# Batch 2's queries and keys turned by transposing DMAs instead of TensorE, with a new order of all engines

## The chip, the cores and the metric

The kernel runs on one core of one Trainium2 chip. The metric is the device time in microseconds (us) of one execution. Engines are named as the profile names them: PE is TensorE's matmul stream and PEld its weight loads, DVE is VectorE, ACT is ScalarE, POOL is GpSimd (which here only issues loads from HBM), SP is SyncE (which issues the other DMAs).

## What is computed

An attention with a local window and a few global keys, and behind it a gated long convolution that takes its result as input. There are B = 4 batches, 8 heads, S = 768 positions and D = 64 values per head; the first 8 keys are seen by every query, and beside them each query sees itself and the 95 keys before it. The masked scores carry a bias that falls with distance, with a slope for each head.

```python
scores = scale * np.matmul(q, k.transpose(0, 1, 3, 2))
...
keep = is_global | is_local
dist = np.where(is_global & ~is_local, float(n_local), np.abs(rel))
scores = np.where(keep, scores - slopes[:, None, None] * dist, -1e9)
a = np.exp(scores - max); a = a / sum(a)
x = (a @ v), heads joined to 512 columns
...
proj = x @ w_proj                       # 512 -> 3 * 512
x1, x2, x3 = the three parts of proj
x2_conv = irfft(rfft(x2, axis=1) * rfft(filter_fft, axis=0))
out = (x1 * x2_conv * x3) @ w_out
```

The lines above are shortened; inputs are cast to 16-bit floats on the way in and the output is 32-bit.

## The kernel before, in words

**Attention of one batch.** The scores need queries and keys with the 64 values of a head on the partitions, while they lie in HBM with positions in the rows. They are loaded as rows and then turned. `QT` (line 759 reads it, with `KT`) holds the turned queries, 128 rows for each pair of heads; `KT` holds seven key tiles of 8 global and 120 local keys each. `scores` (L741) makes, for a pair of heads and one of three groups of key tiles, the scores in two PSUM banks; ACT takes their exponential (L774) and DVE multiplies with a mask that holds the bias and the window (L791). `values` (L794) multiplies with the values, which carry a column of ones for the sum; DVE takes the reciprocal, and DVE or ACT scales the result into `xn` (L833 on DVE; L837 on ACT, one small instruction for each tile and head). `transpose_x` (L843) turns it on PE (L854), and DVE or ACT copies it out of PSUM to `xT` (`copy`, L314).

**Gated convolution of one batch.** `gate` (L922) makes two of the projections (L932), `butterfly` (L861) folds `xT`, `conv` (L981) projects (L993) and carries the transform by matmuls with tables (`spectra` L1117, L1124; back at L1023), and the output projection (L1059) goes by ACT to `ot` and from there by SP to HBM (L1070).

**Two ways to turn queries and keys.** Batches 1 and 2 go the first way, batch 3 the second; batch 0 goes a variant of the first.

- On PE: `load_pair` (L358) loads, head by head, 96 KB at a time, so 16 loads for a batch. `turned` (L697) makes six 128x128 transposes of a head pair into one bank (L707), and then a copy by ACT or DVE brings it out: one copy of 128x768 for queries, and three for keys (128x720, 128x120, and 128x56 for the global ones). A batch has four pairs, so eight such steps and 48 transposes.
- By DMA: `load_tiles` (L379) loads rows of all heads, six query tiles of 128 KB and seven key tiles of 120 KB, and two SP copies (kn<-kn) repeat the eight global keys in every tile. `cross` (L396) then issues 13 transposing DMAs on SP (L406), one for a tile, which write `QT` and `KT` directly. The names are TILES and CROSS; both are (3,).

`QT`, `KT` and the row buffers `qn`, `kn` exist once, the value buffer `vn` twice. So rows of batch b + 1 can only be loaded where rows of batch b were turned, and `QT` and `KT` only be written where the scores of the batch before were made. `load_v` (L411) loads the values in seven row tiles; when the first of them is there, `load_global` (L418) copies its eight global rows to the other tiles with two DMAs on SP (vn<-vn), which `values` waits for.

**Order.** Every operation is recorded with its engine or engines, its cost and what it reads and writes. `schedule` (L156) then takes the order from a string written out by hand: each word is the number of an operation, the letter of its engine (P, A, V for DVE, G for POOL, S for SP) and its PSUM banks. `248G` is the load of the first value tile of batch 1, `249S` the copy of its global rows. Where an operation may go to ACT or DVE, the letter decides. Each engine runs its words in that order, and a word that waits holds up the words of its engine behind it. DMAs too are issued in the order of POOL's and of SP's words.

Of the kernel before, what the change touches and what calls it, by code (L numbers as in the profile page):

```python
# [17 lines left out]
P = 128  # L18
# [23 lines left out]
0V 1V 2A 3G 45S 30A 47S 4V 34V 6A 9A 32G 56S 49S 5V i1b5 22P0 55G 23A 54G 7G 24A 10V 17P1 8V 33V 25V 51G 18A  # L42
35G 19A 12P2 13A 46V 52G 37A 48V i2b5 83P0 38A 53G 81P3 72G 20V 26A 61G 63G 21A 14V 44V 50V 15V 39V 201P1 93P2
36V 87P4 84A 202V 57V 60G 43A 82A 207V 95P3 16A 94A 97P67 209V 85P2 65G 64G 29V 11V 62G 88A 41V 91P0 203V 66G
96V 149P45 239G 42A 236G 86V 98A 204A 234G 150A 40V 89P3 121P67 151P45 238G 58V 208V 90V 205V 122A 152A 117P23
92V 99P67 206V 103P45 211V 233G 212V 118A 213V 235G 100A 119P23 101P67 153P01 104A 105P45 120A 102A 154A 27V
214V 115P23 237G 106V 215V 59S 116A 107V 155P67 78A 216V 110P01 111V 128P23 232G 157P45 156A 77A 217V 67G
220P6 112V 162P01 221A 158V 108P6 73A 113P7 129V 130V 123P23 109A 224P6 159V 131P4 114V 79A 222P7 245G 68G
341P5 241G 243G 225A 163V 124V 76A 223A 218P6 31V 240G 164V 125V 337P0 132V 28V 339P1 244G 340V 165P7 126P4
127V 247G 160P2 74A 335P1 338A 137P4 342A 166V 193V 139A 161V 133P7 376P23 219A 242G 336V 246G 354P45 414P01  # L50
377A 138P6 69G 167P2 355A 134P3 415A 183V 135A 184V 351P45 352A 192V 194V 140V 373P01 186V 185V 136V 343P6
374A 459G 169A 248G 195V 172P7 70G 71G 171P4 464G 187V 196V 173A 226P01 347P2 227A 345P3 411P45 251G 344V 252G
353V 349P0 145P6 75A 174V 249S 412A 348V 141P2 346V 254G 357P45 350V 228A 417P01 147A 375V 253G 420P67 188V
168P3 255G 197V 458G 256G 470G 356V 189V 143A 170V 142P2 465G 418A 471G 144V 175P0 358A 146P1 421A 382P67 198V
191V 460G 360P23 177A 413V 199V 148V 80A 190V 383A 379P45 380A 258P0 463G 361A 259A 229P67 416V 200V 378V
271P1 363P45 272A 230A 422V 275P2 461G 364V 273P3 231A 250S 466G 276A 284P6 419V 385P01 362V 274A 384V 286P7
359V 260P2 386V 365V 387V 462G 560P3 287A 479G 478G 285A 469G 261A 368P45 381V 279P0 366P1 472G 561A 473G 369V
468G 277P2 288V 423P67 370V 280A 262P3 289V 264P0 278A 367A 371P1 424V 263A 467G 425V 372A 282V 566P2 428P45
266P1 390P67 257G 265A 706G 567A 562P0 281V 267A 429V 388P3 391V 563A 179P2 430V 564P1 392V 176P4 181A 180P0
565A 389A 269V 576P67 268V 182V 178V 426P1 577A 431P2 393P0 432V 427A 394V 579P45 687G 580A 598P67 639P23 640A  # L60
396P0 698G 572P1 574P4 270V 395P5 298P2 407P3 696G 573A 599A 474G 397A 450V 570P1 568P6 449V 451V 695G 452V
404P5 575A 299A 408P7 694G 409A 403P4 571V 684G 398V 636P23 585P01 453V 410V 690G 569A 283V 454V 405A 600V
637A 582P67 445P4 480G 586A 481G 699S 399P2 447A 406V 433P3 446P4 455V 477G 702G 292P5 583A 435A 401A 456V
457V 645P67 607P01 448V 693G 293A 300P3 638V 646A 290P2 294P5 441P4 295A 304P6 442P5 581V 476S 608A 482G 584V
443A 400P7 475S 578V 302P4 697G 296P0 609V 688G 301A 291A 647V 303A 444V 689G 402V 485P1 604P45 297A 305A 587V
642P23 486A 307V 306V 605A 601P67 641V 691G 643A 685S 483P0 496P1 593P23 602A 308V 594V 603V 497A 484A 498P4
606V 588P67 487P5 589V 683G 701G 499A 595A 437P4 309V 489P0 590V 490A 488A 704G 310V 615P67 439A 692G 644V
311V 703G 610P23 611V 616V 700S 653P01 491P5 617A 438P4 612V 312V 511P2 440V 654V 686S 434P3 313V 596P4 618P6
512A 597A 492A 619A 500P7 655V 591P2 592A 613P5 314V 493V 501A 502P4 509P6 494V 648P01 504P7 656P2 705G 614A
624P5 510A 787S 649V 505A 513V 657A 632P6 503A 436V 315V 620P7 507V 629P4 621P3 626A 323P5 495V 506V 789S 514V  # L70
625P2 650A 508V 785S 634A 622A 651P0 324A 652A 628P6 784S 515P7 786S 517P5 529P1 518A 623V 527P3 627V 316V
675V 523P0 516A 528A 519P2 630A 670P5 525P3 793S 526A 521P7 633P6 530A 520A 791S 332P3 674V 317P2 524A 635V
333A 631V 672A 662P3 522A 803P45 790S 677V 806P67 800P01 318A 664A 801A 788S 676V 326P2 804A 795S 532V 327A
329P3 320P0 678V 330A 321A 796S 707P2 679V 663P3 807A 797P01 531V 680V 794S 825P67 533V 708A 534V 822P45 798A
682V 826A 720P2 666P0 535V 805V 536V 665V 671P3 823A 537V 681V 828P67 673V 721A 819P45 711P1 658P3 668A 820A
712A 799V 792S 829A 724P2 861P01 827V 870P67 660A 867P45 725A 722P3 540V 538V 802V 319S 334S 871A 733P2 868A
539V 723A 709P6 809P45 726P3 541V 734A 808V 554P7 331S 872V 810V 727A 735P3 542P2 830V 811V 862A 863V 555A
710A 814P01 836P45 864P67 736A 815V 543A 824V 837V 667P3 816V 865A 659P2 869V 838A 866V 715P6 713P7 661V
878P01 325S 669V 714A 548P2 728P7 812P3 879V 716A 821V 880V 737V 817P6 831P45 729A 873P01 839P7 322S 832V 730V
818A 813A 874V 551P3 731V 833A 875V 328S 732V 718V 557P6 881P4 738V 834P5 876P0 545P1 840A 835A 882A 877A  # L80
856P7 556S 717V 841P4 904V 741P0 903V 719V 745P5 546A 749P1 558A 742A 843A 549A 746A 857P6 842P0 906V 905V
907V 908V 851P2 858A 909V 750A 753P7 559S 844A 747P5 754A 739P4 743P1 751P0 883P7 744A 912P1 748A 910V 740A
852P4 752A 756V 859A 755V 913A 924P6 853A 936P2 552A 925A 911V 884P5 757V 854A 938P6 914P3 845V 937A 758V
916P2 939A 915A 860V 928P3 759V 888P6 210A 917A 760V 553S 940V 761V 929A 920P4 550S 918P3 886A 919A 926P2 941V
764V 921A 923V 922V 932P3 889P5 927A 898P4 933A 930P3 544S 894P2 885A 946P7 931A 762V 896A 942P3 935V 957P1
846P2 934V 855V 947A 958A 961P7 943A 944P1 962A 948P3 945A 763V 959P0 949A 963P7 960A 964A 765V 951V 950V
847P1 781P0 547S 891A 965V 966V 952V 967V 769P5 899P7 848A 953V 770A 900A 968V 954V 969V 772P2 955V 970V 956V
766P3 849A 773A 971V 850V 974V 774S 901A 972V 893P2 767A 782A 975V 775P7 973V 890A 892V 778P3 771S 895A 897V
982P2 768S 985V 779A 902V 783S 976P3 887V 776A 979P7 986V 983A 987V 993P2 989P6 988V 780S 994P 1001P0 980V
990P 777S 977A 978S 997P7 998P 995A 984S 991A 999A 1002P 1003V 981S 996S 992S 1000S 1004S  # L90
# [24 lines left out]
class Plan:  # L115
# [7 lines left out]
    def op(self, eng, cost, fn, r=(), w=(), acq=(), use=(), nbytes=0, table=None, name="",  # L123
# [21 lines left out]
        for b in use:  # L145
            b.left += 1
            b.users.append(o)
            p.add(b.owner)
# [50 lines left out]
class Fused:  # L199
# [6 lines left out]
    PAIR_G = ()  # L206
    VD = 96
    FIRST = (("k",0),("q",0),("k",1))
    TILES = (3,)
    CROSS = (3,)  # L210
# [27 lines left out]
    def buffers(self):  # L238
# [35 lines left out]
        self.ab = [t(f"ab{i}", [P, 3, DM]) for i in range(2)]  # L274
        self.X = t("X", [P, 6, DM])
        pp = t("pp", [P, 2, 4, DM])
        self.p1, self.p2 = ([pp[:, x, 2 * i:2 * i + 2] for i in range(2)] for x in range(2))
# [9 lines left out]
        self.ot = [t(f"ot{i}", [P, DM], F32) for i in range(6)]  # L287
# [555 lines left out]
    def transpose_x(self, j, c):  # L843
# [5 lines left out]
        def run(_):  # L849
            tx = b.f16()  # L850
            for i in range(2):
                for n, t in enumerate(ts):
                    o = step * i + KL * n
                    nc.tensor.transpose(tx[:, o:o + P], self.xn[j][:, i, t], self.ident)  # L854
        g.op("P", 0.0558 * 2 * len(ts), run, acq=[b], r=[("xn", j, c), "ident"], name="trx")
        dst = self.xT[:, 2 * j:2 * j + 2, self.Q0[c]:self.Q0[c] + W]
        g.op("AV", {"A": act(2 * W), "V": dve(2 * W, 2, True)}, lambda e: self.copy(
            e, dst, b.f16()[:, 0:2 * step].rearrange("p (i w) -> p i w", i=2)[:, :, 0:W]), use=[b],
            w=[("xT", j, c)], name="xT")
# [89 lines left out]
    def attention(self, b):  # L949
# [5 lines left out]
        for c in range(3):  # L955
# [8 lines left out]
            for j in range(2):  # L964
                self.values(j, c, b % 2)
                self.transpose_x(j, c)
# [14 lines left out]
    def conv(self, b):  # L981
        nc, g, DM, S = self.nc, self.g, self.DM, self.S
        h, last = S // 2, b == self.B - 1
        g.batch = (self.PERIOD * b, self.PERIOD)
        X, y, w = self.X, self.y, self.w
        for i in range(2):
            for t, (src, key) in enumerate((
                    (self.xo[:, i], ("xo",)), (self.xs[:, 3 * i], ("xe", "xd")), (self.xs[:, 2 - i], ("xe", "xd")))):
                bk = g.bank()
# [308 lines left out]
```

## Time and profile before

| | us |
|---|---|
| median of 3 runs | 165.75 |
| lowest, highest | 165.38, 165.85 |
| span of the profiled execution | 163.0 |
| median less that span | 2.75 |
| PE busy | 154.0 |
| DVE busy | 151.6 |
| ACT busy | 150.3 |
| POOL busy | 76.8 |

The profiled execution has no other time of its own than its span. Busy time of PE counts a matmul until its modelled end, so PE at 10 of 10 us needn't be PE at its peak. The page names groups of instructions by source line and by tiles: `KT<-bank` is a copy from a PSUM bank to `KT`. Issues of DMAs on POOL and SP have their own rows; "us to landing" is from the issue to the last byte. Queue q0 carries POOL's DMAs and q1 SP's.

### The profile page before, as it was taken

To read this page: it belongs to the slowest core of one execution; us is meant where nothing else is said; L and a number is where in the kernel's file an instruction comes from. 1 tells how busy PE (TensorE), PEld (TensorE's weight loads), DVE (VectorE), ACT (ScalarE), POOL (GpSimd) and SP (SyncE) were. 2 spreads that over 40 slices of the span, in tenths; PEclk is the share of its full clock that TensorE was granted. 3 is DMA by queue.
4 is the path that set the end of the run, shared out by engine and by line. 5 is a ranking of instruction groups with operands and counts; after the bars stand their busy time and mean duration, and the time that the engine had idled before them with its cause. 6 is when DMAs were issued, how large, how long until landed. Compare 5 with 4: busy or idle time off the path is not lost.

```text
span 163.0 us, 4256 instructions
## 1 busy us (share of the span) xinstructions
PE 154.0 (94%) x1604; PEld 94.7 (58%) x1604; DVE 151.6 (93%) x356; ACT 150.3 (92%) x327; POOL 76.8 (47%) x101
## 2 busy tenths in 40 slices
PE   6599997999999999999999999999999999999980
PEld 2274355866655777666577584445676664584440
DVE  6599699999999999999999999999999999999960
ACT  8999996999999999999999999999998999997850
POOL 7999199999979997999970000000000000000000
PEclk9999999999999999999999999999999999999999
DMA  5999999999999999999999964630100106000684
GB/s 170 200 166 164 165 150 138 147 158 174 190 162 154 139 136 136 149 153 163 161 129 162 134 121 101 236 150 0 64 4 6 66 0 253 5 4 0 264 332 178
DMA packets 84956, 21.95 MB, mean 135 GB/s; under 512 B 75584, under 2 KB 81992, under 8 KB 84936
## 3 DMA queue, kind: packets, MB, share of 16 engines
q0 software_dynamic: 73040, 12.11, 98.4%
q1 hardware_dynamic: 11896, 9.57, 21.4%
q8 instruction: 12, 0.20, 0.5%
q14 instruction: 8, 0.07, 0.1%
HBM read 25.40 MB, written 6.29 MB: 194 GB/s over the span
## 4 chain that ended last, share of the span: by engine, by line
PE 85%; ACT 9%; DVE 3%; issue 1%
PE bank L932 26%; PE bank L993 13%; PE bank L1059 13%; PE bank L759 7%; PE bank L854 4%; PE bank L809 4%; PE bank L707 3%; PE bank L1023 3%; PE bank L1124 3%; PE bank L814 3%; PE bank L753 2%; ACT E L774 2%; ACT KT L314 1%; PE bank L1030 1%; PE bank L690 1%; ACT QT L314 1%
## 5 line engine op out<-in xcount | busy, mean ns | idle before, releaser
L932 PE MATMUL bank<-xT,w 128*128 128x384 f16 x256 | 48.2, 326 | 0.0
L774 ACT ACTIVATE E<-bank 128x864 f16<-128x864 f32 x48 | 41.0, 911 | 0.3 <-PE bank L759 0.2
L932 PEld LDWEIGHTS <-w 128*128 128x128 f16 x256 | 23.9, 98 | 15.8 <-issue 0.3
L339 POOL DMA_DIRECT2D vn<-in_v_dram x28 | 26.3, 979 | 1.1 <-DMA w<-in_moe_w_proj_dram 1.1
L339 POOL DMA_DIRECT2D kn<-in_k_dram x25 | 21.8, 892 | 5.4 <-DMA vn<-in_v_dram 4.0
L1059 PE MATMUL bank<-wo,y 128*128 128x512 f16 (+1 forms) x100 | 22.6, 371 | 0.0
L339 POOL DMA_DIRECT2D qn<-in_q_dram x25 | 21.8, 885 | 0.1
L791 DVE TENSOR_TENSOR E<-E,mask 128x864 f16<-128x864 f16 x36 | 20.3, 591 | 0.0
L318 ACT ACTIVATE x<-bank 128x384 f16<-128x384 f32 x32 | 16.6, 547 | 0.0
L318 ACT ACTIVATE ot<-bank 128x512 f32<-128x512 f32 (+1 forms) x23 | 13.3, 610 | 3.5 <-PE bank L1059 3.1
L809 PE MATMUL bank<-vn,E 128*128 128x65 f16 x224 | 15.3, 193 | 0.9 <-DVE xn L833 0.7
L993 PE MATMUL bank<-w,xs 128*128 128x512 f16 x64 | 15.9, 379 | 0.0
L809 PEld LDWEIGHTS <-E 128*128 128x128 f16 x224 | 14.0, 97 | 2.3 <-DMA vn<-in_v_dram 0.4
L1059 PEld LDWEIGHTS <-y 128*128 128x128 f16 x100 | 9.5, 98 | 9.9 <-DVE y L1113 0.5
L814 PE MATMUL bank<-vn,E 128*128 128x65 f16 x192 | 15.0, 193 | 0.0
L314 ACT CAST eo<-bank 128x384 f16<-128x384 f32 x32 | 14.3, 513 | 0.6 <-PE bank L1030 0.2
L314 ACT CAST X<-bank 128x512 f16<-128x512 f32 x24 | 14.3, 636 | 0.4
L314 ACT CAST ab<-bank 128x512 f16<-128x512 f32 x24 | 14.3, 629 | 0.4 <-PE bank L993 0.3
L833 DVE TENSOR_TENSOR xn<-bank,rc 128x512 f16<-128x512 f32 (+1 forms) x19 | 14.3, 771 | 0.1
L814 PEld LDWEIGHTS <-E 128*128 128x128 f16 x192 | 13.1, 97 | 1.9 <-issue 1.2
L759 PE MATMUL bank<-QT,KT 64*128 64x216 f16 (+2 forms) x224 | 13.7, 242 | 0.0
L759 PEld LDWEIGHTS <-KT 64*128 64x128 f16 x224 | 7.9, 94 | 8.7 <-issue 6.8
(163 smaller groups left out, 334.1 us busy)
## 6 DMA issues: line engine op xcount, KB each, us to landing
out_dram<-ot SPq DMA_DIRECT2D x23, 256.0 KB
vn<-in_v_dram POOLq DMA_DIRECT2D x28, 120.0 KB, 7.6
kn<-in_k_dram POOLq DMA_DIRECT2D x16, 96.0 KB, 5.1
qn<-in_q_dram POOLq DMA_DIRECT2D x16, 96.0 KB, 5.2
w<-in_moe_w_proj_dram POOLq DMA_DIRECT2D x4, 256.0 KB, 5.8
kn<-in_k_dram POOLq DMA_DIRECT2D x7, 120.0 KB, 6.2
g<-in_moe_filter_fft_dram POOLq DMA_DIRECT2D x1, 768.0 KB, 10.6
qn<-in_q_dram POOLq DMA_DIRECT2D x6, 128.0 KB, 7.0
```

Source lines behind the costliest of these rows:

```text
L314: {"A": nc.scalar.copy, "V": nc.vector.tensor_copy, "G": nc.gpsimd.tensor_copy}[e](out, in_)
L318: self.nc.scalar.mul(out, in_, c)
L339: return self.g.op(eng, 0.57 + 0.00035 * nbytes[0] if eng == "G" else 0.5, lambda _: e.dma_start(dst, src), w=w, r=r, nbytes=nbytes, name= ...
L759: nc.tensor.matmul(bs[hh].f32()[:, off:off + w], self.KT[hs, hp, P * m:P * m + P], self.QT[hs, hp, KL * m:KL * m + w], start=(off == 0 and ...
L774: g.op("A", act(864), lambda _: nc.scalar.activation(eo, bs[0].two()[:, :, 0:432].rearrange("p h (m w) -> p h m w", m=2), Act.Exp, scale=s ...
L791: g.op("V", dve(864, 2), lambda _: nc.vector.tensor_mul(eo, eo, mk), r=[("mask", 2 * hp), ("mask", 2 * hp + 1)], w=[("E", hp, gi)], name=" ...
L809: nc.tensor.matmul(o[:, n, hh], ef[:, at:at + P], vt[:, t, 2 * hp + hh, 0:D + 1], start=first, stop=(t == 0), skip_group_check=True)
L814: nc.tensor.matmul(o[:, n, hh], ef[:, at:at + P], vt[:, t - 1, 2 * hp + hh, 0:D + 1], start=False, stop=True, skip_group_check=True)
L833: nc.vector.tensor_mul(to, o[:, :, :, 0:D], rc.to_broadcast([P, 2, 2 * nt, D]))
L932: nc.tensor.matmul(bk.f32()[:, 0:h], self.w[:, c, o + P * j:o + P * j + P], self.xT[:, c, h * s:h * s + h], start=(c == 0), stop=(c == 3))
L993: nc.tensor.matmul(bk.f32(), src[:, c], w[:, c, DM:2 * DM], start=(c == 0), stop=(c == 3))
L1059: nc.tensor.matmul(bk.f32()[:, 0:n], y[:, c, P * t:P * t + P], self.wo[:, c, cs], start=(c == 0), stop=(c == 3))
```

## The change

TILES and CROSS become (2, 3). Batch 2's queries and keys are then loaded by rows (13 loads instead of 16, with two more kn<-kn copies), and turned by 13 more transposing DMAs on SP. Its eight `turned` steps go: 48 transposes, four copies to `QT` and four times three copies to `KT`. The string ORDER is new throughout: operations are numbered anew from the first load of batch 2 on, they stand in another order on every engine, have other banks, and some go to the other of ACT and DVE:

| operation | ACT, before to after | DVE, before to after |
|---|---|---|
| kT (copies to KT) | 7 to 1 | 5 to 7 |
| qT (copies to QT) | 6 to 3 | 6 to 5 |
| xT | 17 to 22 | 7 to 2 |
| xn | 5 to 6 | 19 to 18 |
| ab (line 314, from L993's bank) | 24 to 23 | 0 to 1 |

Some small work on tables at the start changes hands too. The rest of the diff adds options (PAIR_AB, PAIR_X, PAIR_EO, PAIR_OT, PAIR_T, WHOLE) that join two banks in one copy or several products in one instruction; all of them are empty, so that `conv`, `spectra` and `transpose_x` issue the same instructions as before.

```diff
 ORDER = """
-0V 1V 2A 3G 45S 30A 47S 4V 34V 6A 9A 32G 56S 49S 5V ...
...
-374A 459G 169A 248G 195V 172P7 70G 71G 171P4 464G 187V ...
-353V 349P0 145P6 75A 174V 249S 412A 348V 141P2 346V 254G ...
...
+272A 357P45 273P1 416V 413V 362V 421A 384V 358A 248G 286P0 ... 276A 460S 249S
...
-    TILES = (3,)
-    CROSS = (3,)
+    TILES = (2, 3)
+    CROSS = (2, 3)
...
-            b.users.append(o)
-            p.add(b.owner)
+            p.add(b.owner)
+            if "P" not in cost:
+                p.update(x for x in b.users if "P" in x.cost)
+            b.users.append(o)
```

The last hunk is in `Plan.op`: an operation that is not PE's and uses a bank is recorded as coming after every PE operation that uses this bank. `460S` is the first of the new kn<-kn copies.

Among POOL's loads the first value tile of batch 1 (`248G`) is the 34th before and the 39th after. The loads of batch 2's rows are the 36th, the 38th, the 40th, 41st and 43rd, and the 47th to 55th save the 54th. SP issues `460S`, `249S` and `250S`, another kn<-kn copy, and then the 13 transposes of batch 2, without any other DMA between them.

More of the change, by code (lines that the diff above doesn't have):

```diff
@@ L47 @@
[L47 to L51, printed above, removed]
@@ L286, in buffers @@
         self.x1 = [self.x1p[:, i] for i in range(4)]
-        self.ot = [t(f"ot{i}", [P, DM], F32) for i in range(6)]
+        self.otp = t("ot", [P, 6, DM], F32)
+        self.ot = [self.otp[:, i] for i in range(6)]
         self.fl = self.gt[1].rearrange("p a b -> p (a b)").rearrange("p (a b) -> p a b", a=6)
@@ L847, in transpose_x, with run @@
         b = g.bank()
[L849 to L859, printed above, removed]
+        for n, j in enumerate(js):
+            def run(_, n=n, j=j):
+                tx = b.f16()
+                for i in range(2):
+                    for m, t in enumerate(ts):
+                        o = step * (2 * n + i) + KL * m
+                        nc.tensor.transpose(tx[:, o:o + P], self.xn[j][:, i, t], self.ident)
+            g.op("P", 0.0558 * 2 * len(ts), run, acq=() if n else [b], use=[b] if n else (),
+                 r=[("xn", j, c), "ident"], name="trx")
+        k = 2 * len(js)
+        dst = self.xT[:, 2 * js[0]:2 * js[0] + k, self.Q0[c]:self.Q0[c] + W]
+        g.op("AV", {"A": act(k * W), "V": dve(k * W, 2, True)}, lambda e: self.copy(
+            e, dst, b.f16()[:, 0:k * step].rearrange("p (i w) -> p i w", i=k)[:, :, 0:W]), use=[b],
+            w=[("xT", j, c) for j in js], name="xT")
     def butterfly(self, js):
@@ L985, in conv @@
         X, y, w = self.X, self.y, self.w
[L986 to L989, printed above, removed]
+        units = [(i, t, src, key) for i in range(2) for t, (src, key) in enumerate((
+            (self.xo[:, i], ("xo",)), (self.xs[:, 3 * i], ("xe", "xd")), (self.xs[:, 2 - i], ("xe", "xd"))))]
+        pair = b in self.PAIR_AB
+        for u in range(0, 6, 1 + pair):
+            bks = [g.bank() for _ in range(1 + pair)]
+            for bk, (i, t, src, key) in zip(bks, units[u:]):
                 def proj(_, src=src, bk=bk):
@@ L1031, in turn @@
                                          start=False, stop=True, skip_group_check=True)
-                    g.op("P", pe(*[P] * (6 if apart else 4)), turn, acq=[bk], r=src + [
-                        ("inv", s) for s in range(7)], name="inv")
+                    g.op("P", pe(*[P] * (6 if apart else 4)), turn, acq=[bk] if not both else () if par else both,
+                         use=[bk] if both and par else (), r=src + [("inv", s) for s in range(7)], name="inv")
+                    if both and par == 0:
+                        continue
+                    if both:
+                        g.op("AV", self.evac(2 * h), lambda e, eo=eo, jj=jj, both=both: self.copy(
+                            e, eo[:, jj], both[0].two()[:, :, 0:h]), use=both, w=[ke + (jj, 0), ke + (jj, 1)],
+                            name="eo", after=self.early if b == 0 else ())
+                        continue
                     g.op("AV", self.evac(h), lambda e, eo=eo, jj=jj, par=par, bk=bk: self.copy(
@@ L1052, in conv, with project @@
             m = 2 if last and t == 5 else 1
+            if (b, t // 2) in self.PAIR_OT:
+                if t % 2 == 0:
+                    both = [g.bank(), g.bank()]
+                def project(_, t=t, bk=both[t % 2]):
+                    for c in range(4):
+                        nc.tensor.matmul(bk.f32(), y[:, c, P * t:P * t + P], self.wo[:, c],
+                                         start=(c == 0), stop=(c == 3))
+                g.op("P", pe(*[512] * 4), project, acq=() if t % 2 else both, use=both[1:] if t % 2 else (),
+                     r=[("y", i, t // 3) for i in range(2)] + ["wo"], name="out")
+                if t % 2 == 0:
+                    continue
+                g.op("AV", self.evac(1024), lambda e, o=o, both=both: self.times(
+                    e, self.otp[:, o - 1:o + 1], both[0].two(), osc), use=both, w=[("ot", o - 1), ("ot", o)], name="ot")
+                g.op("S", 0.5, lambda _, o=o, t=t, b=b: nc.sync.dma_start(
+                    self.out[b, P * t - P:P * t + P].rearrange("(x p) n -> p x n", p=P), self.otp[:, o - 1:o + 1]),
+                    r=[("ot", o - 1), ("ot", o)], nbytes=(256, 2048))
+                g.bias = 0.0
+                continue
             for x in range(m):
@@ L1115, in gated, with parts, products @@
              r=ys + [("g", b % 2, j, half) for j in range(js.start, js.stop)], w=ys, name="y*g")
+    def parts(self, b):
+        self.spectra(b, (2, 3))
+        if b in self.WHOLE:
+            self.products(b, (0, 1, 2, 3))
+        self.spectra(b, (4, 5))
     def spectra(self, b, pair):
-        nc, g, X, DM = self.nc, self.g, self.X, self.DM
-        n = pair[0] // 2
-        for s in pair:
-            bk = g.bank()
+        nc, g, X = self.nc, self.g, self.X
+        join = b in self.PAIR_X
+        bks = [g.bank() for _ in pair]
+        for x, s in enumerate(pair):
             i, t = (s // 2, 1 + s % 2) if s < 4 else (s - 4, 0)
             table = self.fold[:, (s + 2) % 4] if s < 4 else self.fwd[:, s]
+            bk = bks[x]
             g.op("P", pe(512), lambda _, bk=bk, i=i, t=t, table=table: nc.tensor.matmul(
-                bk.f32(), table, self.ab[i][:, t], start=True, stop=True), acq=[bk], name="fwd",
+                bk.f32(), table, self.ab[i][:, t], start=True, stop=True),
+                acq=[bk] if not join else () if x else bks, use=[bk] if join and x else (), name="fwd",
                 r=[("ab", i, t), ("fwd", 1) if s > 3 else "foldp"])
-            g.op("AV", self.evac(512), lambda e, s=s, bk=bk: self.copy(e, X[:, s], bk.f32()),
-                 use=[bk], w=[("X", s)], name="X")
-        xs = X[:, pair[0]:pair[0] + 2]
+            if not join:
+                g.op("AV", self.evac(512), lambda e, s=s, bk=bk: self.copy(e, X[:, s], bk.f32()),
+                     use=[bk], w=[("X", s)], name="X")
+        if join:
+            g.op("AV", self.evac(1024), lambda e: self.copy(e, X[:, pair[0]:pair[0] + 2], bks[0].two()),
+                 use=bks, w=[("X", s) for s in pair], name="X")
+        if pair[0] == 4 or b not in self.WHOLE:
+            self.products(b, pair)
+    def products(self, b, pair):
+        nc, g, X, DM = self.nc, self.g, self.X, self.DM
+        n, m = pair[0] // 2, len(pair) // 2
+        xs = X[:, pair[0]:pair[0] + 2 * m]
         if n == 2:
@@ L1152, in sums @@
         def sums(_):
-            nc.vector.tensor_sub(xs[:, 0], p1[:, 0], p2[:, 1])
-            nc.vector.tensor_add(xs[:, 1], p1[:, 1], p2[:, 0])
-        g.op("V", 2 * dve(512, 2), sums, r=[("p1", k), ("p2", k)],
+            x, y, z = two(xs), two(p1), two(p2)
+            nc.vector.tensor_sub(x[:, :, 0], y[:, :, 0], z[:, :, 1])
+            nc.vector.tensor_add(x[:, :, 1], y[:, :, 1], z[:, :, 0])
+        g.op("V", 2 * dve(512 * m, 2), sums, r=[(k, n + x) for k in ("p1", "p2") for x in range(m)],
              w=[("X", s) for s in pair], name="sums")
```

141 lines of the change are left out of this document (76 added, 65 removed).

## The prediction, made before the changed kernel was run

> **What bounds the kernel now.** I read the page first (busy shares, then the 40 slices), then the chain of work that ended last, then busy time by stretches of 10 us.
>
> ```profile
> span 163.0 us, 4256 instructions
> PE 154.0 (94%) x1604; PEld 94.7 (58%) x1604; DVE 151.6 (93%) x356; ACT 150.3 (92%) x327; POOL 76.8 (47%) x101
> DMA  5999999999999999999999964630100106000684
> PE 85%; ACT 9%; DVE 3%; issue 1%
> ```
>
> Three engines are busy for over nine tenths of the span, and the chain runs over PE for 85% of it. The stretches say where this is so (columns: length, then busy time and count of PE, PEld, DVE, ACT, POOL, then clock, DMA share, GB/s).
>
> ```profile
> 10.00:20.00 10.00, 9.87 (x119) 4.85 (x116) 8.29 (x28) 9.91 (x17) 5.97 (x8) 1.00 1.51 163
> 40.00:50.00 10.00, 10.00 (x99) 5.85 (x97) 10.00 (x30) 10.00 (x17) 8.75 (x11) 1.00 1.94 175
> 50.00:60.00 10.00, 10.00 (x156) 7.41 (x155) 9.97 (x22) 9.83 (x23) 10.00 (x13) 1.00 2.24 142
> 90.00:100.00 10.00, 10.00 (x85) 6.49 (x83) 10.00 (x20) 9.76 (x31) 0.00 (x0) 1.00 0.93 123
> 150.00:163.00 13.00, 8.51 (x45) 4.02 (x42) 7.38 (x22) 6.37 (x13) 0.00 (x0) 0.99 0.64 243
> ```
>
> From 40 to 100 us PE has no gap at all, DVE next to none, at the full granted clock (1.00). So time taken from PE there is time gained, but only as far as DVE gives the same amount back: it is co-bound. Up to 90 us the DMA engines are full too (9 in nearly every slice), and POOL, which issues the loads, is 10.00 busy from 50 to 60 us. Before 20 us DVE has room (8.29 of 10).
>
> The profiled execution spans 163.0 us; the median of the runs is 165.75 us. I take the 2.75 us between them as lying around the span, and carry it unchanged.
>
> **The change part by part.**
>
> *Turning leaves PE.* The 48 transposes of batch 2's queries and keys stand in the chain like this (start, length, what):
>
> ```profile
> 52.58 0.34 PE bank L707 x6
> ...
> 65.51 0.67 PE bank L707 x12
> ```
>
> That is 56 ns each, 48 x 56 ns = 2.7 us, all between 52.58 and 66.18 us, where PE has no idle time. PE: **-2.7 us**.
>
> *Evacuations and the shuffle between ACT and DVE.* The rows below give mean ns of one behind the comma.
>
> ```profile
> L314 ACT COPY KT<-bank 128x720 f16<-128x720 f16 x7 | 5.6, 799 | 0.0
> L314 ACT COPY QT<-bank 128x768 f16<-128x768 f16 x6 | 5.2, 867 | 0.0
> L314 DVE COPY KT<-bank 128x720 f16<-128x720 f16 x5 | 3.4, 671 | 0.0
> L314 DVE COPY QT<-bank 128x768 f16<-128x768 f16 x6 | 4.1, 686 | 0.3 <-PE bank L710 0.2
> L314 DVE COPY xT<-bank 128x480 f16<-128x480 f16 x4 | 1.6, 400 | 0.0
> L314 DVE COPY xT<-bank 128x576 f16<-128x576 f16 x3 | 1.4, 451 | 0.0
> L833 DVE TENSOR_TENSOR xn<-bank,rc 128x512 f16<-128x512 f32 x12 | 8.0, 673 | 0.0
> L833 DVE TENSOR_TENSOR xn<-bank,rc 128x768 f16<-128x768 f32 x7 | 6.6, 940 | 0.0
> ```
>
> Batch 2's eight evacuations go: four queries and three keys on ACT, one key on DVE. In the new order ACT does one key evacuation where it did seven, and three query evacuations where it did six. Counting the main copies alone that is 6 x 0.80 + 3 x 0.87 = 7.4 us off ACT, and it is given other work for it: five copies of xT and one large xn come from DVE. DVE by count: keys 5 to 7 (+1.3 us, +0.4 each for the narrow copies that go with one, my estimate, so +2.1), queries 6 to 5 (-0.7), xT 7 to 2 (three of 0.40, two of 0.45: -2.1), xn 12 to 13 of the small and 7 to 5 of the large (+0.7 - 1.9), and one ab copy (about +0.6, taken from the xn row of the same width). Sum: **-1.3 us** on DVE. Some small table work of the set-up moves to it as well, into the first 20 us, where the row above shows room; uncovered it would cost under 1 us.
>
> So before any new wait the gain lies between DVE's 1.3 and PE's 2.7 us. I take **2.4**, near PE's end, because the chain gives PE 85% and DVE 3%. By the DVE end it is 1.3.
>
> *Loads and their order.* Sixteen head-wise loads of 96 KB become thirteen row-tile loads of 120 or 128 KB: 1.54 MB become 1.61 MB, and POOL issues 82 loads for 85, at some 0.9 us each 2.7 us less. POOL's busy time bounds nothing by itself, but its order does. The first row tile of batch 1's values was the 34th load; it becomes the 39th. SP copies its first eight rows into the other tiles (the vn<-vn copies of load_global), and `values` of batch 1 needs those copies.
>
> ```profile
> 36.08 1.05 POOL L339 DMA_DIRECT2D vn<-in_v_dram  x1
> ...
> 39.31 4.68 POOL L339 DMA_DIRECT2D vn<-in_v_dram  x5
> ```
>
> ```profile
> 41.79 1.43 SPq L339 DMA_DIRECT2D vn<-vn  x2
> ```
>
> ```profile
> vn<-in_v_dram POOLq DMA_DIRECT2D x28, 120.0 KB, 7.6
> ```
>
> ```profile
> q1 hardware_dynamic: 2, 0.00, 0.2%
> ```
>
> ```profile
> q1 hardware_dynamic: 19, 0.02, 14.6%
> ```
>
> ```profile
> 48.55 0.23 PE L809 MATMUL bank<-vn,E 128*128 128x65 f16 x2
> ```
>
> The tile was issued at 36.08 and SP went on at 41.79. The two q1 rows are of the stretches 42:46 and 46.5:47: the copies moved nothing up to 46 and ran at 47, so the first, 24 KB, took about 5.1 us from issue to end (41.79 to 46.9) amid full DMA engines. PE began at 48.55: some 1.6 us to spare. In the new order the tile takes the slot of the second of the five loads at 39.31, that is an issue at 40.2, a landing at 47.8 by the median of 7.6, and a copy done at 47.8 + 5.1 = 52.9. Adding up, in the new order, the intervals that PE's same instructions took before puts PE at these matmuls at 50.2. Wait: **2.7 us** by that row; 0 if the copy moved at once, more if the load comes later. Behind the waiting matmul stand all of PE's later work and, after one or two instructions, DVE's and ACT's. DVE works on meanwhile: it sat idle only 0.1 us before all 19 xn instructions,
>
> ```profile
> L833 DVE TENSOR_TENSOR xn<-bank,rc 128x512 f16<-128x512 f32 (+1 forms) x19 | 14.3, 771 | 0.1
> ```
>
> so when values end it is still behind by about one such, 0.8 us. I take **+1.9 us** as paid, with 0 and 4 as ends.
>
> A rule speaks against this wait: the Trainium skill, "DMA: Bandwidth & Descriptors", section "Queues, rings and completion order", says that each DMA engine goes round-robin between the queue rows that have work, packet by packet. By that rule SP's small copy would not sit behind POOL's loads, the wait would be near nothing, and the time that of rival A; the two q1 rows, with nothing for 4 us behind the issue, do not bear it out.
>
> *The crossbar.* Thirteen more transposing DMAs stand on SP, now while loads run. Before, they began at the end of the loads.
>
> ```profile
> 77.28 9.71 SPq L406 DMA_TRANSPOSE QT<-qn  x3
> 87.09 2.52 SPq L406 DMA_TRANSPOSE KT<-kn  x2
> ...
> 96.95 3.83 SPq L406 DMA_TRANSPOSE KT<-kn  x3
> ```
>
> ```profile
> 80.00:81.00 1.00, 1.00 (x17) 0.64 (x16) 1.00 (x4) 1.00 (x4) 1.00 (x2) 1.00 2.47 171
> 81.00:82.00 1.00, 1.00 (x7) 0.57 (x6) 1.00 (x3) 1.00 (x7) 1.00 (x2) 1.00 2.39 116
> 82.00:83.00 1.00, 1.00 (x27) 0.82 (x25) 1.00 (x3) 1.00 (x6) 1.00 (x2) 1.00 1.23 83
> 84.00:88.00 4.00, 4.00 (x40) 2.50 (x37) 3.93 (x8) 4.00 (x15) 0.41 (x1) 1.00 2.40 151
> ```
>
> SP issues one in 1.26 us (2.52 / 2). The first scores of batch 2 need five of them; their tiles are loads 36 to 43 of the new order, so they are issued from about 50.3 to 57.2, and with the 4 us that the first one took (issued 77.28, moving until 83) the fifth is there at about 61. PE gets there, by the same sum as above, at 59.4 to 62. So this is 0 to 1.6 us, and whatever PE has already waited at the values comes off it: I add nothing. The last key tile follows at about 71 against a need at 70 to 72; again 0 to 1.
>
> What a transpose costs the loads: in two microseconds of its run (81:83) the rate fell from the 151 GB/s of 84:88 to 116 and 83, that is 35 + 68 = 103 KB fewer, 0.7 us of load time each. The ends are 0, if it takes only gaps, and 1.26 us, if the loads stand while SP issues it. Thirteen make 9.1 us by the row, and POOL's 2.7 us of saved issues come off: 6.4. The loads of batch 3 that follow end at 84.4 now:
>
> ```profile
> 82.59 1.82 POOL L339 DMA_DIRECT2D vn<-in_v_dram  x2
> ```
>
> ```profile
> 100.54 0.73 PE L759 MATMUL bank<-QT,KT 64*128 64x216 f16 x12
> ```
>
> Batch 3's scores begin at 100.54, and in the new order its thirteen transposes have some 6 us to spare, by the same sums. So by the row the shift is just hidden, and I take **0**; rival B prices it if it is not.
>
> By another line, "TRN2 transpose DMAs are as fast as regular DMAs" (the Trainium skill, "Advanced Engine Details and Errata", section "X-Bar Transpose (TRN2)"), thirteen would cost the loads little, and rival B below would fall; the 83 GB/s of 82:83 speaks against it.
>
> **Sum.** -2.4 + 1.9 = -0.5 us on the span: 162.5, and with 2.75 around it **165.2 us**.
>
> **Rivals.**
>
> A, *the cover is whole*. The copies or the tile land earlier than in the row (the DMA engines' mix is another), PE waits nowhere, and the 2.4 to 2.7 us are paid out: 163.1 to 163.4 us; with half of the wait 164.3. For it: in the trace before, the same copies were in time, by 1.6 us. Against it: five loads ahead of the tile.
>
> B, *the DMA path becomes the bound* (slower). The thirteen transposes push back the loads, and POOL's later loads, which wait for a qn or kn tile to be turned before it is written again, push back batch 3. It decides where a transpose takes from the loads more than (6 + 2.7) / 13 = 0.67 us, so the row's 0.7 lies at the edge. At 0.9 the thirteen take 11.7 us, 3.0 of it uncovered: 165.2 + 3.0 = 168.2 us; at 0.75 it is 1.0 us, 166.2; at the end of 1.26, 7.7 us, 172.9. For it: the DMA row full until 90 us, and 151 falling to 83. Against it: one transpose only is seen among loads, in a stretch in which POOL still issued.
>
> C, *DVE is the bound and PE's time was never the price*: the gain is 1.3, the wait at the values takes 1.3 or a little more of it: 165.7 us, no change. For it: DVE 10.00 in 40:50 and 90:100. Against it: 3% of the chain.
>
> That the crossbar isn't used is no rival: the instruction lists show 96 PE rows (48 transposes and their weight loads) fewer and 13 DMA transposes more.
>
> **How the numbers follow.** Forecast, a small gain or a draw, 164.4 to 166.0 us: chance 0.36 (0.20 of it faster by over 0.3%, 0.10 within, 0.06 slower). A, 163.1 to 164.4: 0.23. B, 166.0 to 170: 0.33, of which 0.07 above 168.3. C, 0.08 (within 0.07, slower 0.01). 0.3% is 0.5 us and about what a measurement of this kernel can tell from no change. So faster 0.43, same 0.17, slower 0.40. As cases of both signs hold most of the chance, the range goes from A's 163.2 to B's 168.3; beyond it I leave 0.07 above and 0.05 below, and the rest of the 0.2 for what is in no case here.
>
> **What would show it.** PE: no L707 between 52 and 66 us, and 2.7 us less busy time. At 50 to 53 us a wait of the L809 weight loads for the vn<-vn copies: 1 to 3 us if I am right, none in A. SP: thirteen L406 between 50 and 67 us, each landing some 4 us behind its issue; a slow one shows as PE waiting at L759 for KT or QT. POOL's last load: before 87 us in the forecast, past 90 in B, with a second wait at L759 past 100 us. DVE's busy time down by about 1.3 us. The forecast is wrong if the values' copies come before 50 us, or if batch 3's scores wait.

## The result, and the profile after

The changed kernel takes 179.94 us (median of 4 runs, 177.76 to 179.99) against 165.67 us before on the same chips (4 runs): a ratio of 1.086, 95% interval 1.079 to 1.093. The forecast was 165.2 us, and the range ended at 168.3. The profiled execution took 179.98 us, 178.2 of them span, so 1.8 us lie around the span (the prediction had 2.75); the loss is inside. Times are medians over all executions of a kernel; the ratios leave out the few slow ones, those over 1.5% above the fastest of their kernel.

The page of the changed kernel, the rows that answer to those shown of before:

```profile
span 178.2 us, 4214 instructions
PE 157.9 (89%) x1556; PEld 93.2 (52%) x1556; DVE 152.2 (85%) x368; ACT 147.4 (83%) x313; POOL 75.6 (42%) x98
PE   7787968999999989901999999999999999999990
DMA  5999999999999999999999999981021030040574
PE 59%; DMA 21%; DVE 8%; SPq 6%; ACT 2%; issue 2%; DVEq 0%; ACTq 0%
```

The 48 transposes are gone (1604 matmuls became 1556), but the chain now runs over DMA and SP's queue for 27% where it had none of either. PE's row has a hole in its 18th and 19th slice, about 76 to 85 us, and is thin in the first seven. The DMA engines stay full some 20 us longer. The stretches (columns as in the prediction) give the two places:

```profile
10.00:20.00 10.00, 8.31 (x92) 3.73 (x88) 5.81 (x22) 8.31 (x12) 6.99 (x9) 0.83 1.38 157
20.00:30.00 10.00, 7.85 (x95) 3.70 (x94) 9.59 (x27) 7.95 (x13) 9.90 (x13) 1.00 2.26 156
...
70.00:80.00 10.00, 5.55 (x52) 3.25 (x49) 8.94 (x17) 5.78 (x13) 2.93 (x4) 1.00 1.69 129
80.00:90.00 10.00, 5.82 (x24) 2.24 (x24) 1.53 (x3) 3.05 (x4) 5.30 (x7) 0.51 2.65 135
```

In 70:90 PE works 11.4 of 20 us, and in 80:90 it does so at a granted clock of 0.51, so that even in those busy microseconds it got less done. (Lines of the changed file stand some eight further down: L767 is the scores, L817 the values, L414 the transposing DMAs, L347 the loads, L326 and L328 scaled copies.) What PE waits for there, in PE's timeline:

```profile
81.99 0.36 PE L767 MATMUL bank<-QT,KT 64*128 64x216 f16 x2 [6.45 <-DMA QT<-qn]
84.55 0.68 PE L767 MATMUL bank<-QT,KT 64*128 64x168 f16 x8 [2.19 <-DMA KT<-kn]
```

Batch 2's last scores wait for the last two of the 13 transposes. The chain between 53 and 85 us shows how these came to be so late (start, length, what), and SP's timeline shows the first and the last of them:

```profile
53.19 9.69 DMA kn<-in_k_dram
62.91 1.70 SPq L414
...
70.84 13.66 DMA KT<-kn
```

```profile
49.76 1.85 SPq L414 DMA_TRANSPOSE QT<-qn  x1
...
70.84 3.42 SPq L414 DMA_TRANSPOSE KT<-kn  x1
```

A load of a key tile took 9.7 us. SP issued the 13 transposes close behind one another, but 1.76 us apart on the mean ((70.84 - 49.76) / 12), where the prediction had 1.26; the trace does not tell whether an issue was long because it waited for its tile or for room in the queue. The last transpose took 13.7 us from issue to landing. Before, loads of row tiles had a median of 6 to 7 us, and the one transpose among loads, issued at 77.28, moved until 83: 5.7 us.

The thin first slices are another thing. DVE's longest wait in the set-up:

```profile
DVE inr L328 <- ACT inv L326: 3.7, 1, 3.7
```

DVE copies a table out of a PSUM bank (207V) that ACT also reads (205A). In the new list 205A stands first, so DVE waits for it, and on ACT it is queued behind exponentials that wait for PE.

### The profile page after: what moved, and what is told of

Same layout as the page of the kernel before. It is cut to its first block, busy times and chain, and to the rows that moved or that the text cites. A ratio compares the mean times of both kernels' runs of the same rounds, so it can differ in the third digit from the quotient of the medians.

```text
span 178.2 us, 4214 instructions
## 1 busy us (share of the span) xinstructions
PE 157.9 (89%) x1556; PEld 93.2 (52%) x1556; DVE 152.2 (85%) x368; ACT 147.4 (83%) x313; POOL 75.6 (42%) x98
## 4 chain that ended last, share of the span: by engine, by line
PE 59%; DMA 21%; DVE 8%; SPq 6%; ACT 2%; issue 2%; DVEq 0%; ACTq 0%
PE bank L942 16%; DMA KT<-kn 13%; PE bank L1007 11%; PE bank L1100 11%; DMA kn<-in_k_dram 5%; SPq L414 5%; PE bank L767 5%; DMA h<-in_q_dram 3%; PE bank L1172 2%; PE bank L862 2%; PE bank L817 2%; PE bank L822 2%; PE bank L1038 2%; DVE KT L322 1%; PE bank L715 1%
## 5 line engine op out<-in xcount | busy, mean ns | idle before, releaser
L942 PE MATMUL bank<-xT,w 128*128 128x384 f16 x256 | 50.3, 329 | 0.0
L347 POOL DMA_DIRECT2D vn<-in_v_dram x28 | 25.9, 932 | 10.3 <-DMA g<-in_moe_filter_fft_dram 3.0
L767 PE MATMUL bank<-QT,KT 64*128 64x216 f16 (+2 forms) x224 | 15.7, 256 | 10.4 <-DMA QT<-qn 7.3
L347 POOL DMA_DIRECT2D kn<-in_k_dram x24 | 21.7, 908 | 5.0 <-DMA KT<-kn 1.8
L347 POOL DMA_DIRECT2D qn<-in_q_dram x23 | 20.4, 893 | 7.0 <-DMA vn<-in_v_dram 6.8
L1100 PE MATMUL bank<-wo,y 128*128 128x512 f16 (+1 forms) x100 | 23.3, 371 | 0.0
L956 DVE TENSOR_TENSOR g<-bank,x 128x384 f16<-128x384 f32 x24 | 13.2, 550 | 9.6 <-PE bank L942 9.5
L767 PEld LDWEIGHTS <-KT 64*128 64x128 f16 x224 | 8.1, 98 | 21.6 <-issue 16.1
L326 ACT ACTIVATE x<-bank 128x384 f16<-128x384 f32 x32 | 17.2, 551 | 0.8 <-PE bank L942 0.7
L1007 PE MATMUL bank<-w,xs 128*128 128x512 f16 x64 | 17.0, 395 | 0.0
L326 ACT ACTIVATE ot<-bank 128x512 f32<-128x512 f32 (+1 forms) x23 | 14.4, 640 | 2.5 <-PE bank L1100 2.3
L322 ACT CAST X<-bank 128x512 f16<-128x512 f32 x24 | 14.3, 618 | 2.3 <-PE bank L1172 2.2
L817 PE MATMUL bank<-vn,E 128*128 128x65 f16 x224 | 15.1, 193 | 0.4 <-DVE KT L322 0.3
L817 PEld LDWEIGHTS <-E 128*128 128x128 f16 x224 | 14.0, 97 | 1.9 <-issue 0.4
```

What stands on the lines that cost most here:

```text
L322: {"A": nc.scalar.copy, "V": nc.vector.tensor_copy, "G": nc.gpsimd.tensor_copy}[e](out, in_)
L326: self.nc.scalar.mul(out, in_, c)
L347: return self.g.op(eng, 0.57 + 0.00035 * nbytes[0] if eng == "G" else 0.5, lambda _: e.dma_start(dst, src), w=w, r=r, nbytes=nbytes, name= ...
L767: nc.tensor.matmul(bs[hh].f32()[:, off:off + w], self.KT[hs, hp, P * m:P * m + P], self.QT[hs, hp, KL * m:KL * m + w], start=(off == 0 and ...
L817: nc.tensor.matmul(o[:, n, hh], ef[:, at:at + P], vt[:, t, 2 * hp + hh, 0:D + 1], start=first, stop=(t == 0), skip_group_check=True)
L942: nc.tensor.matmul(bk.f32()[:, 0:h], self.w[:, c, o + P * j:o + P * j + P], self.xT[:, c, h * s:h * s + h], start=(c == 0), stop=(c == 3))
```

## Experiments

Two theories. **Theory 1**: the 13 transposes, issued among loads, come too late and hold back the loads. **Theory 2**: the new order loses the time, with or without transposes. The kernel before ran on the same chip beside each of the groups below (164.6 to 165.0 us); ratios are to it.

### Without batch 2's transposes

```diff
-... nc.sync.dma_start_transpose(out, src[:, n])
+... b == 2 or nc.sync.dma_start_transpose(out, src[:, n])
```

> The changed kernel without the 13 transposing DMAs of batch 2, all else as it is; batch 2's scores are made from what QT and KT hold from batch 1. Theory 1 (the transposes, issued among loads, come too late and hold back the loads; PE waits for them at 76 to 85 us): that wait of about 9 us, the slow clock behind it and the late loads go, the set-up's loss of 4 us stays: 166 to 169 us. Theory 2 (the new order itself loses the time, with or without transposes): over 175 us.

Measured: 167.99 us, ratio 1.018 (1.012 to 1.024). Against 179.94 that is 12 us (11 by the two ratios), so theory 1 has most of the loss. But with turning free the new order is still 3.3 us slower than before; theory 2 has that part. PE's timeline shows one piece of it:

```profile
54.54 0.22 PE L817 MATMUL bank<-vn,E 128*128 128x65 f16 x2 [1.38 <-DMA vn<-vn]
```

This is the wait that the prediction gave 1.9 us: batch 1's values for the copies of the global rows.

### The set-up's wait mended

```diff
-28V 205A 99P45 117P23 100A 207V 41V
+28V 99P45 117P23 100A 207V 205A 41V
```

> The changed kernel with one word moved: 205A, ACT's copy of a table out of a bank, stands behind 207V and not before it in the list, so that DVE's copy out of the same bank no longer waits for ACT's (3.7 us in the trace); the order on each engine stays. If the 4 us that batch 0's values are late come from this wait: 3 to 4 us earlier values of batch 0, and 176 to 178 us if that lead is kept up to the end, no gain if it is lost again in the wait for the transposes (179 to 180), as theory 1 has it where the landing of the loads sets that wait. Theory 2 wants 175 to 177.

Measured: 179.39 us, 1.088 (1.083 to 1.094): no gain. The lead is there, and then lost:

```profile
20.00:30.00 10.00, 9.63 (x143) 5.42 (x140) 9.78 (x23) 9.12 (x15) 10.00 (x13) 1.00 2.22 153
50.00:60.00 10.00, 7.44 (x65) 3.94 (x63) 6.53 (x15) 5.04 (x11) 8.53 (x10) 0.83 2.24 156
```

PE has 9.63 busy microseconds in 20:30 where it had 7.85, and waits in 50:60 instead: 2.56 us at 53.95, for the copies of batch 1's global rows, where it had no wait in the changed kernel. Behind that it waits for batch 2's transposes as before. While PE waits for DMAs that land no earlier, coming earlier only makes its wait longer.

### Loads held until batch 2 is turned

POOL's order behind batch 2's last query load (470G); the planner's rule that puts batch 2's value loads ahead of the transposes is dropped for it.

```diff
-470G 477G 476G 473G 480G 257G 481G 478G 479G 680G ... 692G 691G
+470G 692G 691G 473G 476G 477G 478G 479G 480G 481G 257G 680G ...
```

> The changed kernel with another order of POOL's loads only: behind batch 2's last query load come the two loads of batch 3 that wait for the last transposes of batch 2, and then the value loads of batch 2, wo and the rest of batch 3. So POOL holds its loads until batch 2 is turned. Theory 1: with nothing beside them the 13 transposes run at SP's 1.26 us each, the last one lands before 72 us and not at 84.5, PE's wait before batch 2's last scores goes, and the time is 168 to 173 us, with a new wait for batch 2's late values. Theory 2: no better than the changed kernel, or worse by the held loads (180 to 188).

Measured: 182.8 us, 1.108 (1.102 to 1.115). The time is a miss for theory 1, and lies in theory 2's range; of theory 1's mechanism the first half came. The loads were held, SP issued the last transpose only a microsecond earlier, but it landed before POOL went on at 73.13 and not at 84.5, about 3 us behind its issue where it took 13.7 among loads:

```profile
70.06 1.22 SPq L414 DMA_TRANSPOSE KT<-kn  x1
```

```profile
73.13 0.98 POOL L347 DMA_DIRECT2D kn<-in_k_dram  x1 [15.14 <-DMA KT<-kn]
```

PE's wait before batch 2's last scores is gone. The 15.1 us that POOL stood come back at batch 3: there PE waits 8.1 us for turned keys, works 5.6 us of 100:110, and its clock falls to 0.50 from 108 us on.

```profile
PE bank L767 <- DMA KT<-kn: 8.1, 3, 4.3
```

```profile
100.00:110.00 10.00, 5.59 (x55) 3.63 (x52) 9.93 (x21) 5.94 (x15) 0.00 (x0) 0.86 1.84 132
```

So the wait moved from one batch to the next. This doesn't show that a better order of loads and transposes is impossible: with the loads held, the DMA engines moved only 9 GB/s in 72:74.

### The cost by itself: 13 DMAs more in the kernel before

Thirteen DMAs of 128 KB are added to the unchanged order, on SP behind the copies at 41.8 us; nobody waits for their results.

```diff
+for to in free:
+    g.op("S", 1.3, lambda _, to=to: self.nc.sync.dma_start_transpose(to, src), name="extra")
...
-249S 412A 348V 141P2 ... 250S ...
+249S 412A 348V 141P2 ... 250S (the 13 new words) ...
```

> The kernel before, its order kept, with 13 more transposing DMAs of the same size (128x512, from a table in SBUF to unused buffers) on SP from 43 us on, behind the copies of batch 1's global rows. They compute nothing that is used. Theory 1: they take some 13 x 0.7 to 13 x 1.3 us of the loads' time between 43 and 70 us, batch 2's queries and keys land 6 to 12 us later, PE waits for them: 169 to 176 us. Theory 2: nothing waits for them and the time stays within 1 us of 165.7.

Measured: 177.92 us, 1.078 (1.072 to 1.084): even above theory 1's 176, with the old order on all engines. PE now waits for loads, here for batch 2's queries, and its clock falls behind the waits (0.76 in this stretch):

```profile
PE bank L704 <- DMA qn<-in_q_dram: 4.6, 2, 3.0
```

```profile
50.00:60.00 10.00, 5.76 (x54) 3.50 (x52) 4.89 (x11) 4.83 (x9) 4.51 (x6) 0.76 1.76 129
```

With a wait of 2.7 us for a value tile and one of 1.8 us for batch 2's keys, PE's waits for loads come to 9.1 us.

The same as plain copies (`dma_start(to, src)`, 1 KB runs):

> As the kernel before with 13 more transposes from 43 us on, which came to 177.9 us, but with 13 plain copies of the same 128 KB from SBUF to SBUF in their place. If the transposes cost by their bytes alone (theory 1a), the copies hold back the loads as much: 128 KB at the loads' 155 GB/s are 0.8 us each, 11 us in all, 174 to 178 us. If the cost is the transposing itself (theory 1b: small packets through one path, and loads that stand while it switches), the copies cost 0 to 4 us: 165 to 169 us.

Measured: 168.76 us, 1.024 (1.019 to 1.030): inside 1b, at its upper end, so the bytes alone don't make the cost. Either the number of packets or the transposing itself makes the rest. The same copies cut into runs of 256 bytes (both sides strided):

> As the kernel before with 13 plain SBUF copies (2.4% slower, against 7.8% with 13 transposes), but each copy cut into runs of 256 bytes on both sides, 512 runs a copy as a transpose has packets of 256 bytes. If the transposes cost the loads so much because of the number of small packets: as with the transposes, 5 to 9% slower, 172 to 179 us. If it is the transposing itself: as with the plain copies, 1 to 4% slower, 166 to 171 us.

Measured: 174.48 us, 1.060 (1.055 to 1.064). The small runs bring back most of it; some 2% remain that only the transpose has. On the pages, SP's queue q1 has 2256 packets more than before with the plain copies, 6864 more with the copies in 256-byte runs and 7072 more with the transposes. And the transposes again, behind the loads:

> The kernel before with the same 13 extra transposes, put on SP behind the output writes of batch 0, where no loads run any more (from about 106 us); they write dead row buffers. If the cost is contention with the loads: nothing, 165 to 166 us, at 1.26 us each on SP. If such a transpose costs PE, DVE or ACT anything by itself (a shared port or the clock), 167 us or more.

Measured: 164.17 us, 0.996 (0.993 to 0.999): nothing lost. SP took 17.5 us to issue them, and nobody noticed:

```profile
105.78 7.91 SPq L1243 DMA_TRANSPOSE qn<-inv  x6
113.73 9.54 SPq L1243 DMA_TRANSPOSE kn<-inv  x7
```

POOL's last two loads tell the same of all three, in POOL's timelines of the copies, of the copies in 256-byte runs and of the transposes among loads:

```profile
87.44 1.80 POOL L336 DMA_DIRECT2D vn<-in_v_dram  x2
```

```profile
92.38 1.80 POOL L336 DMA_DIRECT2D vn<-in_v_dram  x2
```

```profile
97.03 1.80 POOL L336 DMA_DIRECT2D vn<-in_v_dram  x2
```

Before they began at 82.59. So 13 DMAs put them back by 4.9, 9.8 and 14.4 us: 0.37, 0.75 and **1.11 us each**; the times rose by 4.2, 9.5 and 13.2 us. The end follows the load stream nearly one for one. Not all of the 14.4 us was taken by the transposes: POOL waited 3.1 us for PE, itself late by then, before one load of keys, where before it waited 1.2. The load just ahead of that wait stands 12.6 us back (5.0 and 9.1 with the copies), which makes **0.97 us** for each transpose.

### What the new order would give if turning were free

Starting from the kernel without batch 2's transposes, first the set-up's word moved as above:

> The changed kernel without batch 2's 13 transposes (168.0 us) and with 205A behind 207V in the list. Theory: two things in the new order lose time, the set-up's wait of DVE on ACT (3.7 us) and the late first value tile of batch 1; with only the first mended, PE comes earlier to batch 1's values and waits there longer for the copies of the global rows (1.4 us before): 166 to 168 us, so little gained. If the set-up is all that the new order loses: 164 to 165 us.

Measured: 166.12 us, 1.009 (1.006 to 1.013). Then the value tile too:

```diff
-... 251G ... 248G ... 460S 249S ... 250S
+... 248G 251G ... 249S 250S 460S ...
```

> As the one before, and the first value tile of batch 1 is loaded four places earlier (248G ahead of 251G), and its two copies stand ahead of the first kn copy on SP. Theory: both losses of the order mended, the wait at batch 1's values goes, and the time is what the prediction had for a whole cover with turning free of cost: 163 to 165 us. If the rest of the order loses time elsewhere: 166 us or more.

Measured: 164.56 us against 164.56, 1.000 (0.997 to 1.002). The two mends give 0.9% and 1.0%, some 1.5 us each, and with both the new order stands where the old one does. The expectation of 163 to 165 holds by its number, but there is no gain in it. A line of the page of this kernel, and a stretch of its set-up:

```profile
PE 152.8 (93%) x1556; PEld 91.8 (56%) x1556; DVE 152.0 (93%) x368; ACT 147.2 (90%) x313; POOL 75.5 (46%) x98
```

```profile
10.00:20.00 10.00, 7.49 (x106) 3.74 (x102) 8.30 (x34) 8.80 (x13) 6.29 (x8) 1.00 1.36 154
```

DVE has 152.0 us of work, where it had 151.6 before. PE's busy time is 1.2 us down (152.8 for 154.0), not 2.7, and in 10:20 PE works 7.49 us where it worked 9.87 before. So part of what turning saves may still be lost in the set-up of the new order; no run separates that.

### Is it PE's time at all that can be gained?

In the kernel before, with its order: `turned` issues nothing for batch 2; five mask multiplications of batch 2 left out; both.

```diff
+b2 = self.b == 2           # in turned: no transposes, no copies
+out = self.b == 2 and 4 * gi + hp < 5     # in scores: no tensor_mul
```

> The kernel before without the turning of batch 2: its 48 transposes and their eight evacuations are left out (PE -2.7 us, ACT -8 us, DVE -1.1 us), and batch 2's scores are made from what QT and KT hold. No transposing DMA takes the place. As the prediction had it (PE bounds): 2.4 to 2.7 us faster, ratio 0.984 to 0.986. If DVE bounds as much as PE: 0.5 to 1.1 us faster, ratio 0.993 to 0.997.

Measured: 163.87 us against 164.95, 0.995 (0.992 to 0.998).

> The kernel before without five of the twelve mask multiplications of batch 2 on DVE (5 x 0.59 = 2.95 us of DVE, nothing of PE); the scores of these heads go unmasked. If PE alone bounds: no change, ratio 0.998 to 1.002. If DVE bounds too but PE as well: up to 1 us faster, ratio 0.994 to 1. If DVE alone: 2.5 to 3 us faster, 0.982 to 0.985.

Measured: 164.71 us, 0.998 (0.995 to 1.001).

> Both of the two before: without batch 2's turning and without five of its mask multiplications (PE -2.7 us, DVE -4.0 us). If PE and DVE are bound together, only this one gains PE's 2.7 us: ratio 0.980 to 0.986, more than the sum of the two alone. If either bounds alone, no more than the better of the two.

Measured: 164.61 us, 0.998 (0.996 to 1.000). Turning for nothing gives 0.5%, not the 1.6% of PE's 2.7 us: the case of the first expectation in which DVE bounds as much as PE. But the third shows that this isn't the reason: without both, PE's and DVE's work together, it is no faster than without the turning alone, where PE and DVE bound together would have given 1.4 to 2%. And the second shows that DVE alone isn't the bound either. In the first kernel PE has gaps where the transposes were while DVE has next to none (first row); with the masks out too, DVE waits later (second row):

```profile
50.00:60.00 10.00, 9.34 (x140) 6.33 (x139) 9.96 (x21) 7.25 (x15) 10.00 (x13) 1.00 2.16 137
```

```profile
70.00:80.00 10.00, 9.69 (x98) 5.77 (x96) 7.24 (x15) 9.84 (x19) 9.68 (x12) 1.00 2.36 161
```

In the second row neither PE nor DVE is full, ACT (9.84) and POOL (9.68) nearly are. Which of ACT, the loads or the fixed order then sets the pace I did not separate; that stays open.

## Why the prediction was wrong, point by point

**The crossbar: the step that failed.** In the sum this step stands at 0, and both of its parts were mis-sized.

*What a transpose costs the loads.* I had 0.7 us, with 1.26 us as the upper end, so that 6.4 us of shift met some 6 us to spare, "just hidden". The row was misread: its GB/s count the bytes of the transpose too. In 81:83 of the kernel before, the two queues moved

```profile
q0 software_dynamic: 792, 0.09, 98.2%
q1 hardware_dynamic: 385, 0.10, 81.9%
```

so the loads (q0) moved 0.09 MB where 151 GB/s make 0.30: 0.21 MB fewer, or 1.4 us of load time. By the extra transposes it is 0.97 to 1.11 us each; at that price the step's own working gives 12.6 to 14.4 us less 2.7 of shift, and 3.9 to 5.7 us uncovered: rival B, and 169 to 171 us.

*When the transposes land.* I let the fifth and the last transpose of batch 2 land 4 us behind their issue, from one measured among loads (5.7 us by its own row, 77.28 to 83), and so gave batch 2's own scores 0 to 1.6 and 0 to 1 us. At the fifth PE waited 0.85 us. But the last took 13.7 us, and before batch 2's last scores PE waited 6.45 + 2.19 us. This is where the changed kernel loses most.

What the sum had no term for is the clock: behind that wait PE worked at 0.51 until about 90 us, which by my estimate cost half of the 5.8 busy us in 80:90, some 3 us.

Rival B had the sign, and that the transposes hold back the loads; it had the place wrong. It let batch 3 pay, and POOL's last load did go out late, at 99.45 us; but PE, held up at batch 2, waited only 0.40 us before batch 3's scores. Only with the loads held did the wait stand there.

**The wait at batch 1's values: right in kind, but not paid in the changed kernel.** 1.9 us predicted, 0 to 4 as ends. Without the transposes the runs with and without the mend differ by 1.0%, 1.6 us, and PE's timeline names the copies; with the set-up's word moved, PE waits 2.56 us for them in the changed kernel. In the changed kernel itself there is no such wait: PE comes to these matmuls at 53.86, late by the set-up's delay, which I had not seen. The Trainium skill's rule of turns between queue rows ("DMA: Bandwidth & Descriptors", "Queues, rings and completion order") would have made this wait near nothing; it was there. Yet the rule fits the shares: in 60:62 of the changed kernel, POOL's queue q0 and SP's q1 moved

```profile
q0 software_dynamic: 931, 0.12, 90.6%
q1 hardware_dynamic: 798, 0.19, 77.5%
```

about as many packets each, where before q0 alone moved 2236 in 54:56:

```profile
q0 software_dynamic: 2236, 0.27, 215.7%
```

If the queues take turns packet by packet, a DMA of many small packets takes most from the loads; the copies in 256-byte runs cost twice the plain ones. So I read that rule as one about shares, not about how soon a small DMA lands. It is a fit, no proof: no run shows whether the packets of the profile are those that the rule counts.

**The set-up: missed.** I counted the table work that moved to DVE (under 1 us, into room) and not the wait that its place in the list adds: DVE for ACT at one bank, 3.7 us in the trace, and 0.9% when it is mended in the kernel without transposes, where it was 2.2 us.

**PE's 2.7 us and the gain of 2.4: wrong.** The 48 transposes went as said, and with them 2.4 us of PE's busy time in the kernel before without turning (154.0 to 151.6). But leaving the turning out gives only 0.5% there, and with the new order nothing. DVE did not lose its 1.3 us: its busy time is 0.6 us up in the changed kernel, and 0.4 us in the kernel without the transposes and with both mends. Rival C, no change, has the number of that kernel, but its reason isn't borne out: five mask multiplications less on DVE gave nothing either. The chain's 85% for PE was not the share of the time that a shorter PE would pay, and what does set the pace stays open.

**The line that spoke against rival B.** "TRN2 transpose DMAs are as fast as regular DMAs" (the Trainium skill, "Advanced Engine Details and Errata", "X-Bar Transpose (TRN2)") is not borne out beside loads: 1.078 against 1.060 for copies in runs of the same size and 1.024 for plain ones. In a stretch without loads the transposes cost this kernel nothing (0.996).

## What to carry to other kernels

When the DMA row is full, price every added DMA as time of the stream, by its packets more than by its bytes, and look for the first instruction that needs the end of that stream; "beside other work" is no cover there. A cheap way to learn the price is to put the bare DMAs into the kernel before, with nobody waiting for them: here that cost 13.2 us without any of the new order, where the changed kernel lost 14.3 in all and some 11 to 12 of them by its transposes. And when a row of one transpose is read for its cost, take the transpose's own bytes out of the rate first. And where several engines are full at once, leave the work out first and measure: where that gives only 0.5%, moving it elsewhere has little to win.

## What the runs showed of the hardware beside this

- A wait of some 9 us was followed by a granted clock of 0.51 in 80:90 and only then by full speed; in the kernel without the transposes there is no such wait and the mean clock of its profiled run is 0.998, against 0.962.
- The transposes took 0.97 to 1.11 us each from the loads, and equal small copies 0.70 to 0.75. The traces show where the difference lies: with the extra transposes the rate of all DMAs fell to 46 to 48 GB/s in 51:53 and to 79 to 85 in 68:70, with loads outstanding; with the small copies no microsecond from 49 to 84 us fell below 132 GB/s.
- Between 74 and 82 us the changed kernel's DMA engines moved 69 to 155 GB/s, in stretches of 2 us, with transposes and loads outstanding; why the rate falls beside transposes no run shows.
